# Attention, then two MLPs: the hi and lo rows of q and k written by ScalarE and VectorE instead of by transfers

## The chip, the cores and the metric

One core of one Trainium2 chip runs the whole program. The metric is device time in microseconds (us); the kernel before takes 1175.57 us, the median of 3 runs (1174.51 to 1176.18).

## What is computed

```python
def _attn_ref(q, k, v):                       # 4 batches, 8 heads, 576 rows, 64 columns
    q_rot, k_rot = rotate(q), rotate(k)       # x1*cos - x2*sin, x1*sin + x2*cos
    scores = 1/sqrt(64) * q_rot @ k_rot.T
    attn = exp(scores - max)
    attn = attn / (sum(attn) + 1e-09)
    return attn @ v
def _moe_ref(x, w_gate, w_val, w_out):        # 2304 rows, 512 -> 1536 -> 512
    return (sigmoid(x @ w_gate) * (x @ w_val)) @ w_out
def _moe2_ref(x, w_in, w_out):                # 512 -> 2048 -> 512
    h = x @ w_in
    return (h * sigmoid(1.702 * h)) @ w_out
```

Attention is computed for 32 heads, its output is the input of the first MLP, and that one's output is the input of the second. Everything is float32.

## The kernel before, in words

The program has an attention stage and, behind it, the two MLPs. The change is in the attention stage alone. It works through 16 pairs of heads (pair 0 to 15). For a pair the tile `x` holds q and k of both heads, transposed: partitions 0 to 63 are the 64 columns of head 0, partitions 64 to 127 those of head 1; of its 1152 columns the first 576 are k for head 0 and q for head 1, the last 576 the other way round (`HALVES` names the two). A second tile `xs` holds the same with the two halves of the head's columns exchanged, as the rotation needs them. The rotation is two products and one sum for each half: `rope_mul` on GpSimd, `rope_add` on GpSimd (on VectorE for pair 1).

TensorE multiplies here in a rounded format (fp32r), so each number is split in a rounded part "hi" and the rest "lo", and the product is hi hi + lo lo + lo hi + hi lo. For this a head has a *stack* of 128 partitions, 64 rows of hi and 64 rows of lo (`X` for head 0, `Z` for head 1). One matmul of the stack with itself gives hi hi + lo lo; a second one takes as its weights q's rows exchanged, lo over hi (`Y` for head 0, `Zs` for head 1), and gives the other two products.

`split_qk(i, n)` makes them for pair i: for each half ScalarE writes the rounded part of all 128 partitions to `X` (line 208), and GpSimd the rest to `Y` (line 209; VectorE for pair 1). Both heads' parts then lie on the partitions that the heads have in `x`, and `stack` (lines 258 to 269) moves them to where the matmuls want them by six transfers from SBUF to SBUF, all issued by SyncE. The last two overwrite parts of `Y` and `X` that earlier ones still read, so they wait for these. For pair 0 the function `first_pair` does the same without transfers.

The work of a pair is cut in 9 units (`scores`, lines 271 to 294): 8 units of 128 queries of one head each, and a ninth with the last 64 queries of both heads. A unit's scores fill one of two PSUM buffers `pss`; VectorE takes the maximum (`nm`, line 293), ScalarE the exponentials (line 308), which frees the buffer. Then TensorE transposes them (lines 367 to 379), VectorE or ScalarE copies the result out of PSUM (lines 352 and 354; `PT_DVE` lists the copies that VectorE makes), and TensorE multiplies with v (line 397).

A slot is the work that is recorded around one unit's scores; slot 9 i + u holds unit u of pair i. What else stands in a slot is set by tables of lags: a step of pair i with lag n stands in slot 9 i + n, or 9 i - n for the steps that prepare a pair (`LOAD`, `LOAD_S`, `ROPE_MUL`, `ROPE_ADD`, `SPLIT`). Each engine takes its instructions in the order in which the slots record them; the list `steps` (line 581) says in which order a slot does its steps. During pairs 3 to 8 one piece of the first weights of the MLP is also decoded in each pair (`Weights.decode`, lines 132 to 138: one instruction on ScalarE, five on VectorE, one on GpSimd).

Of the kernel before, what the change touches and what calls it, by code (L numbers as in the profile page):

```python
# [16 lines left out]
P = 128  # L17
# [9 lines left out]
def f(ap):  # L27
    return ap.bitcast(F32)
# [3 lines left out]
def attention_then_mlps(  # L32
# [130 lines left out]
    def load(i, c=slice(0, 2 * S)):  # L163

        if i not in st:
            st[i] = dict(P={}, x=rp.tile([P, 2 * S], F32, tag="x", name="x", bufs=2))
        nc.sync.dma_start(out=st[i]["x"][:, c], in_=qk[i, 0, :, c])

    def load_swapped(i, n, c=slice(0, S)):
# [29 lines left out]
    def rope_add(i, n):  # L199
        add(i, n, nc.gpsimd if i > 1 else nc.vector)  # L200

    def split_qk(i, n):

        if n == 0:
            new_pair(i)
        c = HALVES[n]
        x, hi, lo = (st[i][n_][:, c] for n_ in ("x", "X", "Y"))
        nc.scalar.activation(hi, x, AF.Copy)  # L208
        (nc.gpsimd if i > 1 else nc.vector).tensor_tensor(lo, x, f(hi), ALU.subtract)  # L209
        if n == 1:  # L210
            stack(i)

    def first_pair():


        k, q = HALVES
        q0, q1 = slice(S, S + TAIL + P), slice(S + TAIL + P, 2 * S)
        lo, hi = slice(0, D), slice(D, P)
        first, others = slice(0, TAIL + P), slice(TAIL + P, S)
        for c, n, c_ in ((k, 0, slice(0, S)), (q0, 1, first), (q1, 1, others)):  # L220
            load(0, c)
            nc.scalar.dma_start(out=cos_sin[:, :, c], in_=cos_sin_t[:, :, c])
# [6 lines left out]
        X, Y, Z, Zs = (st[0][n] for n in ("X", "Y", "Z", "Zs"))  # L229
# [17 lines left out]
        hi_of(Zs[hi], x[hi, k])
        hi_of(Y[hi, k], x[hi, q])
        hi_of(Z[lo, k], x[hi, k])
        hi_of(Z[lo, q], x[hi, q])  # L250
        rest(Z[hi, k], x[hi, k], Zs[hi])
        rest(Z[hi, q], x[hi, q], Y[hi, k])
        nc.vector.tensor_copy(Zs[lo], f(Z[hi, k]))
# [247 lines left out]
    LOAD, LOAD_V = 25, -1
    LOAD_S = {ANY: (17, 17), 1: (20, 18), 2: (19, 17)}
# [5 lines left out]
    PT = {ANY: (3, 3, 5, 4, 6, 9, 8, 8, 8, 9, 11, 10, 10, 10), 0: (2, 3, 6, 6, 6, 8, 7, 8, 9, 7, 11, 12, 9, 10), 1: (3, 3, 6, 7, 7, 9, 7, 9, 8, 7, 10, 12, 9, 10), npairs - 1: (3, 3, 6, 6, 5, 8, 7, 9, 8, 7, 12, 12, 9, 11)}  # L508
    PV_STEPS = [(a, [t]) for a in range(2) for t in range(MAINC + 1)]
    PV_EARLY = (0, 7, 8)  # L510
    PV = {ANY: (8, 10, 10, 11, 11, 13, 13, 15, 15, 15), 0: (7, 10, 10, 11, 11, 12, 12, 14, 14, 15), 1: (9, 10, 10, 11, 11, 12, 13, 14, 14, 15), npairs - 1: (8, 9, 10, 11, 11, 15, 16, 17, 17, 18)}

    FACTORS = {ANY: (4, 9), 0: (7, 9)}
    SPREAD = {ANY: (7, 13), 0: (8, 11)}
# [61 lines left out]
    def slot(G):  # L576
# [126 lines left out]
```

## Time and profile before

| | |
|---|---|
| median of 3 runs | 1175.57 us |
| the profiled execution | 1179.7 us |
| its span, from the first to the last instruction | 1177.9 us |
| attention stage, to the first matmul of the MLPs | 337 us |
| MLPs | 841 us |
| busy in the span | TensorE 96%, VectorE 63%, ScalarE 37%, GpSimd 27% |

How to read the rows further down: times are in us unless a row says ns. PE is a matmul on TensorE and PEld its weight load, DVE is VectorE, ACT ScalarE, POOL GpSimd, SPq the queue of SyncE, which issues the transfers. `out<-in` names tiles, without buffer numbers. PEclk is the TensorE clock that the chip granted, 1.00 being 2.4 GHz and 0.50 being 1.2 GHz. A stretch is given as start:end from the start of the span.

### The profile page before, as it was taken

The page shows a single profiled execution, that of the slowest core. Times are in us where ns is not written, and L with a number is a line of the kernel's source. Part 1 is how long each engine was busy: PE and PEld are TensorE (multiplying, and loading weights), DVE is VectorE, ACT ScalarE, POOL GpSimd, SP SyncE. Part 2 cuts the span into 40 slices and gives each one's busy share as a digit, 9 for nine tenths or more (in the row PEclk, how much of TensorE's full clock was granted, in tenths as well). Part 3 has the DMA queues.
Part 4 walks back from the last instruction along what each step waited for, and adds up shares of the span by engine and source line. Part 5 has one row for each costly group of instructions (what it writes and reads, how often), then busy time and mean ns, then how long its engine had stood idle before and what let it go on. Part 6 is the DMA issues. An engine that isn't in the chain of part 4 may idle for free.

```text
span 1177.9 us, 15730 instructions
## 1 busy us (share of the span) xinstructions
PE 1130.3 (96%) x6032; PEld 918.7 (78%) x6032; DVE 742.7 (63%) x1298; ACT 431.5 (37%) x926; POOL 316.4 (27%) x291
## 2 busy tenths in 40 slices
PE   2899898899999999999999999999999999999998
PEld 2576666676778888888888888888888888888887
DVE  6469797665746564655546554567667676676744
ACT  4577677676741121211222112332323222232221
POOL 5577778766211110110100102351001010010100
PEclk9899999999999999999999999999999999999999
DMA  4656565645211111111111111111111111111003
GB/s 173 165 141 180 163 175 149 173 123 141 56 39 52 39 51 36 40 51 36 54 36 38 52 37 36 36 36 52 39 36 55 36 53 38 37 54 36 19 36 125
DMA packets 35275, 86.14 MB, mean 73 GB/s; under 512 B 3952, under 2 KB 4976, under 8 KB 35200
## 3 DMA queue, kind: packets, MB, share of 16 engines
q1 hardware_dynamic: 34352, 83.89, 24.5%
q10 hardware_dynamic: 816, 1.18, 0.3%
q8 instruction: 48, 0.79, 0.3%
q14 instruction: 27, 0.22, 0.1%
q0 software_dynamic: 32, 0.07, 0.0%
HBM read 60.49 MB, written 4.72 MB: 55 GB/s over the span
## 4 chain that ended last, share of the span: by engine, by line
PE 84%; DMA 7%; DVE 2%; ACT 2%; SPq 2%; POOL 2%; issue 1%; ACTq 0%; DVEq 0%; POOLq 0%
PE psh L428 42%; PE pso L428 29%; PE ps_x L397 4%; DMA Zs<-X 4%; PE ps_p L367 3%; PE pss L290 3%; DMA X<-Y 2%; PE pss L291 2%; SPq L269 1%; POOL Y L209 1%; DMA xs<-in_qk_dram 1%; DVE nm L293 1%; PE ps_p L379 1%; ACT P L308 0%; ACT X L208 0%
## 5 line engine op out<-in xcount | busy, mean ns | idle before, releaser
L428 PE MATMUL psh<-xhl,w_in 128*128 128x512 f32 (+1 forms) x2400 | 504.2, 368 | 0.0
L428 PEld LDWEIGHTS psh<-xhl,w_in 128*128 128x128 f32 x2400 | 419.4, 189 | 76.0 <-issue 0.5
L442 ACT ACTIVATE sg<-psh 128x512 f32<-128x512 f32 (+1 forms) x140 | 77.7, 555 | 367.4 <-PE psh L428 366.6
L428 PE MATMUL pso<-w_out,g 128*128 128x512 f32 x864 | 202.4, 389 | 0.0
L444 DVE TENSOR_TENSOR gf<-psh,sg 128x512 f32<-128x512 f32 (+1 forms) x140 | 89.1, 636 | 158.6 <-PE psh L428 112.1
L428 PEld LDWEIGHTS pso<-w_out,g 128*128 128x128 f32 x864 | 161.7, 188 | 33.2
L445 ACT ACTIVATE g<-gf 128x512 fp32r<-128x512 f32 (+1 forms) x140 | 82.5, 589 | 244.0 <-DVE gf L444 244.0
L138 POOL TENSOR_TENSOR w_in<-wt,w_in 128x512 fp32r<-128x512 f32 x40 | 51.8, 1294 | 380.5 <-DVE w_in L137 380.5
L446 DVE TENSOR_TENSOR g<-gf,g 128x512 fp32r<-128x512 f32 (+1 forms) x140 | 95.3, 681 | 91.7 <-ACT g L445 91.7
L428 PE MATMUL pso<-g,w_out 128*128 128x512 f32 (+1 forms) x720 | 152.8, 368 | 0.0
L293 DVE TENSOR_REDUCE nm<-pss 128x1 f32<-128x576 f32 x144 | 107.6, 752 | 58.6 <-PE pss L291 58.1
L428 PEld LDWEIGHTS pso<-g,w_out 128*128 128x128 f32 x720 | 125.8, 189 | 22.6
L138 POOL TENSOR_TENSOR w_out<-wt,w_out 128x512 fp32r<-128x512 f32 x28 | 36.2, 1292 | 263.8 <-DVE w_out L137 263.8
L308 ACT ACTIVATE P<-pss,nm 128x576 f32<-128x576 f32 x128 | 95.1, 743 | 30.0 <-DVE nm L293 29.3
L397 PE MATMUL ps_x<-PT,v 128*64 128x256 f32 (+3 forms) x640 | 102.2, 428 | 0.0
L488 DVE TENSOR_TENSOR acc<-pso,acc 128x512 f32<-128x512 f32 x126 | 83.2, 686 | 20.3 <-PE pso L428 18.0
L367 PE MATMUL ps_p<-ident,P 128*128 128x128 f32 x576 | 86.9, 279 | 0.7 <-ACT P L308 0.7
L290 PE MATMUL pss<-X 128*128 128x288 f32 (+3 forms) x176 | 53.5, 330 | 30.6 <-DMA X<-Y 15.5
L473 DVE TENSOR_TENSOR acc<-pso,acc 128x512 f32<-128x512 f32 (+1 forms) x100 | 61.6, 635 | 28.7 <-PE pso L428 28.7
L354 ACT ACTIVATE PT<-ps_p 128x384 f32<-128x384 f32 (+1 forms) x133 | 62.3, 483 | 44.8 <-PE ps_p L367 39.3
L367 PEld LDWEIGHTS ps_p<-ident,P 128*128 128x128 f32 x576 | 71.3, 144 | 2.7 <-ACT P L308 1.0
L290 PEld LDWEIGHTS pss<-X 128*128 128x128 f32 (+1 forms) x176 | 31.9, 181 | 45.5 <-issue 15.0
(63 smaller groups left out, 1057.2 us busy)
## 6 DMA issues: line engine op xcount, KB each, us to landing
raw<-in_moe_w_out_dram SPq DMA_DIRECT2D x28, 512.0 KB, 3.6
xs<-in_qk_dram SPq DMA_DIRECT2D x31, 288.0 KB, 4.2
x<-in_qk_dram SPq DMA_DIRECT2D x15, 576.0 KB, 4.9
raw<-in_moe_w_in_dram SPq DMA_DIRECT2D x16, 512.0 KB, 3.7
raw<-in_moe_w_gate_dram SPq DMA_DIRECT2D x12, 512.0 KB, 3.8
raw<-in_moe_w_val_dram SPq DMA_DIRECT2D x12, 512.0 KB, 3.8
v<-in_v_dram SPq DMA_DIRECT2D x16, 288.0 KB, 3.8
out_dram<-acc SPq DMA_DIRECT2D x18, 256.0 KB, 2.0
```

Source lines behind the costliest of these rows:

```text
L138: lambda: nc.gpsimd.tensor_tensor(w[:, 1, :], f(t), f(w[:, 0, :]), ALU.subtract),
L290: nc.tensor.matmul(ps[:m, n, o : o + w], T[:, q0 : q0 + m], rhs, start=True, stop=False)
L293: nc.vector.tensor_reduce(nm, ps[:, :, :HALF], axis=AX.XY, op=ALU.max, negate=True)
L308: nc.scalar.activation(st[i]["P"][j][:, c : c + S].rearrange("p (n c) -> p n c", n=2), ps[:, :, :HALF], AF.Exp, bias=nm, accum_out=st[i][" ...
L367: nc.tensor.transpose(ps[:, t * P : (t + 1) * P], pt[:, (3 * g + t) * P : (3 * g + t + 1) * P], ident)
L397: nc.tensor.matmul(ps[h * D : (h + 1) * D, :n], vt[r, vc, :], PT[r, pc, :], start=(t == 0), stop=(t == MAINC))
L428: nc.tensor.matmul(ps, l(sl, a), r(sr, a), start=(sl == 1 and a == 0), stop=(sl + sr == 0 and a == n - 1))
L442: nc.scalar.activation(sg, pss[0][:, :wd], AF.Sigmoid, scale=1.0 if kind == 1 else 1.702)
L444: nc.vector.tensor_tensor(gf, pss[-1][:, :wd], sg, ALU.mult)
L445: nc.scalar.activation(g[:, 0, m, :], gf, AF.Copy)
L446: nc.vector.tensor_tensor(g[:, 1, m, :], gf, f(g[:, 0, m, :]), ALU.subtract)
L488: nc.vector.tensor_tensor(a, ps[:, :DM], a, ALU.add)
```

## The change

`split_qk` works head by head and writes each stack in place. For each head and each half ScalarE writes the rounded part of 64 partitions into the stack's hi rows, and VectorE subtracts and writes the rest into the stack's lo rows, which lie on the other 64 partitions. So a pair has four ScalarE instructions of 64x576 instead of two of 128x576, and four subtractions of 64x576 on VectorE instead of two of 128x576 on GpSimd. `stack` and the tile `Y` are gone. What is left for SyncE are q's exchanged copies, `Xs` and `Zs`: two transfers of 64x576 for each head. `first_pair` is written for the new places of the rows. `x` has three buffers instead of two, and is loaded two slots earlier; the four parts of a split stand in four lags (9, 8, 8 and 5 slots ahead of the pair's first). VectorE makes 4 instead of 6 of the 14 groups of copies out of PSUM, and other lags and the order of the steps in a slot are changed.

```diff
     def load(i, c=slice(0, 2 * S)):
-            st[i] = dict(P={}, x=rp.tile([P, 2 * S], F32, tag="x", name="x", bufs=2))
+            st[i] = dict(P={}, x=rp.tile([P, 2 * S], F32, tag="x", name="x", bufs=3))
...
     def new_pair(i):
-        for n in ("X", "Y", "Z"):
+        for n in ("X", "Z"):
             st[i][n] = rp.tile([P, 2 * S], F32R, tag=n, name=n, bufs=2)
-        st[i]["Zs"] = rp.tile([P, S], F32R, tag="Zs", name="Zs", bufs=2)
+            st[i][n + "s"] = rp.tile([P, S], F32R, tag=n + "s", name=n + "s", bufs=2)
...
+    HEADS = (("X", slice(0, D), slice(D, P), HALVES[1]), ("Z", slice(D, P), slice(0, D), HALVES[0]))
+
     def split_qk(i, n):
         if n == 0:
             new_pair(i)
-        c = HALVES[n]
-        x, hi, lo = (st[i][n_][:, c] for n_ in ("x", "X", "Y"))
-        nc.scalar.activation(hi, x, AF.Copy)
-        (nc.gpsimd if i > 1 else nc.vector).tensor_tensor(lo, x, f(hi), ALU.subtract)
-        if n == 1:
-            stack(i)
+        name, hi, lo, q = HEADS[n // 2]
+        T, Ts, x = st[i][name], st[i][name + "s"], st[i]["x"]
+        c = HALVES[n % 2]
+        nc.scalar.activation(T[hi, c], x[hi, c], AF.Copy)
+        nc.vector.tensor_tensor(T[lo, c], x[hi, c], f(T[hi, c]), ALU.subtract)
+        if HALVES[n % 2] == q:
+            nc.sync.dma_start(out=f(Ts[hi]), in_=f(T[lo, q]))
+            nc.sync.dma_start(out=f(Ts[lo]), in_=f(T[hi, q]))
...
-    def stack(i):
-        X, Y, Z, Zs = (f(st[i][n]) for n in ("X", "Y", "Z", "Zs"))
-        for dst, src in (
-            (Z[0:D], X[D:P]),
-            (Z[D:P], Y[D:P]),
-            (Zs[0:D], Y[D:P, 0:S]),
-            (Zs[D:P], X[D:P, 0:S]),
-            (Y[D:P, S : 2 * S], X[0:D, S : 2 * S]),
-            (X[D:P], Y[0:D]),
-        ):
-            nc.sync.dma_start(out=dst, in_=src)
...
-    PT_DVE = ((0, 1), (2, 0), (2, 2), (3, 1), (4, 0), (4, 1))
+    PT_DVE = ((1, 1), (2, 1), (2, 2), (4, 1))
...
-    LOAD, LOAD_V = 25, -1
+    LOAD, LOAD_V = 27, -1
...
-    ROPE_ADD = {ANY: (13, 10), 1: (8, 7), 2: (12, 9)}
-    SPLIT = {ANY: (8, 7), 1: (6, 5), 2: (8, 8)}
+    ROPE_ADD = {ANY: (12, 10), 1: (9, 8), 2: (12, 9)}
+    SPLIT = {ANY: (9, 8, 8, 5), 1: (6, 5, 5, 4), 2: (8, 8, 7, 7)}
...
-            steps = (step_scores, step_pt, step_decode, step_load, step_pv_early, step_pv, step_rope, step_exps, run_later, step_factors)
+            steps = (step_scores, step_decode, step_load, step_rope, step_pt, step_pv_early, step_exps, step_pv, run_later, step_factors)
```

SyncE, the transfers of one pair in the middle of the stage, of the kernel before. `L269` is `stack`; `x` and `xs` are loads of q and k for later pairs, `v` the load of v, `raw` a piece of the MLP's weights:

```order
L167 DMA x<-in_qk_dram 128x1152
L269 DMA Z<-X 64x1152
L269 DMA Z<-Y 64x1152
L269 DMA Zs<-Y 64x576
L269 DMA Zs<-X 64x576
L269 DMA Y<-X 64x576
L269 DMA X<-Y 64x1152
L111 DMA raw<-in_moe_w_gate_dram 128x2x512
```

The same of the changed kernel, where `L216` and `L217` are the copies of q:

```order
L167 DMA x<-in_qk_dram 128x1152
L111 DMA raw<-in_moe_w_gate_dram 128x2x512
L173 DMA xs<-in_qk_dram 128x576 x2
L184 DMA v<-in_v_dram 128x576
L216 DMA Xs<-X 64x576
L217 DMA Xs<-X 64x576
L216 DMA Zs<-Z 64x576
L217 DMA Zs<-Z 64x576
```

Six transfers became four of the smaller size, and the loads of later pairs now stand ahead of them in the queue.

VectorE in the first three slots of pair 10, of the kernel before. `nm` are the maxima that open the slots, `PT` the copies out of PSUM, `sum` the reciprocal of pair 9's sums, `t` the scaling of an output:

```order
L293 TENSOR_REDUCE nm<-pss 128x1
L321 RECIPROCAL sum<-sum 128x5
L293 TENSOR_REDUCE nm<-pss 128x1
L352 COPY PT_2424<-ps_p 64x64 x2
L352 COPY PT_2424<-ps_p 128x4x64 x2
L293 TENSOR_REDUCE nm<-pss 128x1
L352 COPY PT_2424<-ps_p 128x3x128
```

The same slots of the changed kernel, where `L214` are the subtractions for pair 11:

```order
L286 TENSOR_REDUCE nm<-pss 128x1
L214 TENSOR_TENSOR X<-x,X 64x576
L314 RECIPROCAL sum<-sum 128x5
L286 TENSOR_REDUCE nm<-pss 128x1
L214 TENSOR_TENSOR X<-x,X 64x576
L214 TENSOR_TENSOR Z<-x,Z 64x576
L345 COPY PT_2430<-ps_p 128x4x64 x2
L286 TENSOR_REDUCE nm<-pss 128x1
```

Three subtractions now stand between the maxima of units 0, 1 and 2; the fourth stands in slot 4. Two small copies and one larger one went to ScalarE.

## Rows read from the trace of the kernel before

**Rows 1.** TensorE in order of time: the first and last of 16 matmuls marking unit 8.

```profile
34.93 0.19 PE L290 MATMUL pss<-X 128*64 128x64 f32 x1
...
327.30 0.19 PE L290 MATMUL pss<-X 128*64 128x64 f32 x1
```

**Rows 2.** Busy time by engine of some pairs: us, PE, PEld, DVE, ACT, POOL, PEclk, DMA share, GB/s.

```profile
34.93:60.67 25.74, 20.98 (x129) 14.84 (x127) 11.36 (x23) 14.41 (x40) 14.35 (x15) 0.87 0.64 175
60.67:78.18 17.51, 17.30 (x124) 12.05 (x123) 11.15 (x24) 12.99 (x33) 11.86 (x12) 1.00 0.42 97
78.18:96.29 18.11, 17.52 (x131) 12.75 (x129) 15.43 (x30) 13.91 (x35) 13.31 (x14) 1.00 0.61 178
...
115.19:134.12 18.93, 17.72 (x131) 12.73 (x130) 16.23 (x31) 14.04 (x36) 15.07 (x15) 1.00 0.64 177
...
174.46:193.58 19.12, 17.53 (x130) 12.73 (x129) 15.87 (x31) 13.99 (x36) 14.99 (x15) 1.00 0.61 175
...
212.41:231.11 18.70, 17.25 (x130) 12.71 (x129) 11.95 (x26) 13.41 (x34) 13.32 (x14) 1.00 0.59 151
...
270.48:292.20 21.72, 18.90 (x131) 14.31 (x129) 12.04 (x26) 13.58 (x34) 13.35 (x15) 0.92 0.51 125
292.20:309.41 17.21, 17.21 (x130) 12.72 (x129) 11.94 (x26) 13.39 (x34) 6.40 (x9) 1.00 0.38 90
```

**Rows 3.** Chain of work that ended last, around pair 10's start: start, us, what.

```profile
201.07 0.58 ACT X L208
...
201.72 2.80 POOL Y L209 x2
...
207.04 5.75 DMA Zs<-X
212.84 3.19 DMA X<-Y
...
216.17 0.37 PE pss L290
```

**Rows 4.** Waits, stretch 56:300: who waited for whom, us in total, times, longest.

```profile
PE pss L290 <- DMA X<-Y: 12.1, 7, 2.8
POOL Y L209 <- ACT X L208: 19.4, 17, 3.6
```

**Rows 5.** Short stretches around two waits for the stack, columns as in rows 2.

```profile
235.60:239.20 3.60, 3.53 (x17) 3.55 (x18) 0.93 (x3) 1.41 (x3) 1.41 (x1) 0.56 0.36 132
41.50:47.40 5.90, 5.87 (x25) 4.33 (x25) 2.08 (x4) 3.60 (x11) 1.93 (x2) 0.50 0.34 130
```

**Rows 6.** Durations of the operations that move, ns min/median/max or mean.

```profile
L231 DVE TENSOR_TENSOR Z<-x,Zs x1: 755/755/755, 17.8 to 17.8; 64x576 fp32r<-64x576 f32 x1
L230 ACT ACTIVATE Z<-x x2: 664/672/681, 18.4 to 19.0; 64x576 fp32r<-64x576 f32 x2
L208 ACT ACTIVATE X<-x 128x576 fp32r<-128x576 f32 x2 | 1.4, 704 | 0.0
L209 POOL TENSOR_TENSOR Y<-x,X 128x576 fp32r<-128x576 f32 x2 | 2.8, 1415 | 1.9 <-ACT X L208 1.9
L352 DVE COPY PT<-ps_p 128x384 f32<-128x384 f32 x4 | 2.1, 550 | 0.0
L352 DVE COPY PT<-ps_p 64x64 f32<-64x64 f32 x2 | 0.4, 212 | 0.0
```

**Rows 7.** VectorE with both inputs in SBUF: beside GpSimd's work, and (x62) without it.

```profile
L209 DVE TENSOR_TENSOR Y<-x,X x2: 879/1086/1293, 27.0 to 28.5; 128x576 fp32r<-128x576 f32 x2
L135 DVE SCALAR_TENSOR_TENSOR wt<-raw,wt x6: 681/1823/1830, 92.2 to 189.5; 128x512 uint32<-128x512 uint32 x6
L135 DVE SCALAR_TENSOR_TENSOR wt<-raw,wt x62: 691/693/694, 351.1 to 1115.5; 128x512 uint32<-128x512 uint32 x62
```

**Rows 8.** Transfers of 64x576 by SyncE: count, KB each, us to landing.

```profile
Zs<-X SPq DMA_DIRECT2D x15, 144.0 KB, 5.6
Y<-X SPq DMA_DIRECT2D x15, 144.0 KB, 2.3
```

More of the change, by code (lines that the diff above doesn't have):

```diff
@@ L228, in first_pair @@
         x = st[0]["x"]
-        X, Y, Z, Zs = (st[0][n] for n in ("X", "Y", "Z", "Zs"))
+        X, Xs, Z, Zs = (st[0][n] for n in ("X", "Xs", "Z", "Zs"))
         hi_of = lambda dst, src: nc.scalar.activation(dst, src, AF.Copy)
@@ L241, in first_pair @@
         rest(X[hi, k], x[lo, k], X[lo, k])
-        hi_of(Y[hi, q0], x[lo, q0])
+        hi_of(Xs[hi, first], x[lo, q0])
         rest(X[hi, q0], x[lo, q0], X[lo, q0])
-        nc.vector.tensor_copy(Y[lo, q0], f(X[hi, q0]))
+        nc.vector.tensor_copy(Xs[lo, first], f(X[hi, q0]))
         rope(q1, 1, others, nc.gpsimd)
[L247 to L253, printed above, removed]
-        rest(X[hi, q1], x[lo, q1], X[lo, q1])
-        nc.vector.tensor_copy(Y[lo, q1], f(X[hi, q1]))
-        hi_of(Y[hi, q1], x[lo, q1])
-    def stack(i):
-        X, Y, Z, Zs = (f(st[i][n]) for n in ("X", "Y", "Z", "Zs"))
-        for dst, src in (
-            (Z[0:D], X[D:P]),
-            (Z[D:P], Y[D:P]),
-            (Zs[0:D], Y[D:P, 0:S]),
-            (Zs[D:P], X[D:P, 0:S]),
-            (Y[D:P, S : 2 * S], X[0:D, S : 2 * S]),
-            (X[D:P], Y[0:D]),
-        ):
-            nc.sync.dma_start(out=dst, in_=src)
+        hi_of(Z[hi, k], x[hi, k])
+        hi_of(Zs[lo], x[hi, k])
+        hi_of(Z[hi, q], x[hi, q])
+        rest(Z[lo, k], x[hi, k], Z[hi, k])
+        rest(Z[lo, q], x[hi, q], Z[hi, q])
+        nc.vector.tensor_copy(Zs[hi], f(Z[lo, k]))
+        rest(X[hi, q1], x[lo, q1], X[lo, q1])
+        nc.vector.tensor_copy(Xs[lo, others], f(X[hi, q1]))
+        hi_of(Xs[hi, others], x[lo, q1])
     def scores(i, u):
@@ L276, in scores @@
         for h_ in (h,) if j < MAINC else (1, 0):
-            T, Qs = (st[i][n] for n in (("X", "Y"), ("Z", "Zs"))[h_])
+            T, Qs = (st[i][n] for n in (("X", "Xs"), ("Z", "Zs"))[h_])
             m, cols = P, [(0, 0, 0, HALF), (1, 0, HALF, HALF)]
@@ L282, in scores @@
                 q0, k0 = j * P, S
+            qs = HEADS[h_][3].start
             if j == MAINC:
@@ L290, in scores @@
                 nc.tensor.matmul(ps[:m, n, o : o + w], T[:, q0 : q0 + m], rhs, start=True, stop=False)
-                nc.tensor.matmul(ps[:m, n, o : o + w], Qs[:, q0 : q0 + m], rhs, start=False, stop=True)
+                nc.tensor.matmul(ps[:m, n, o : o + w], Qs[:, q0 - qs : q0 - qs + m], rhs, start=False, stop=True)
         nm = st[i]["nm"][:, h, j : j + 1]
@@ L500, in attention_then_mlps @@
     ANY = None
[L501 to L502 removed]
+    LOAD, LOAD_V = 27, -1
+    LOAD_S = {ANY: (17, 17), 1: (20, 17), 2: (20, 18)}
     ROPE_MUL = {ANY: (17, 20, 13, 14), 1: (17, 20, 13, 13), 2: (17, 20, 13, 12)}
[L504 to L505 removed]
+    ROPE_ADD = {ANY: (12, 10), 1: (9, 8), 2: (12, 9)}
+    SPLIT = {ANY: (9, 8, 8, 5), 1: (6, 5, 5, 4), 2: (8, 8, 7, 7)}
     PT_STEPS = [(j, g) for j in range(MAINC) for g in range(3)] + [(MAINC, 0), (MAINC, 1)]
[L508 removed]
+    PT = {ANY: (3, 3, 5, 6, 6, 7, 7, 8, 7, 9, 10, 11, 11, 10), 0: (2, 5, 6, 5, 7, 9, 7, 8, 9, 7, 11, 12, 9, 10), 1: (3, 3, 6, 7, 6, 9, 7, 11, 8, 7, 10, 12, 9, 10), npairs - 1: (3, 3, 6, 6, 5, 8, 7, 9, 7, 7, 12, 13, 10, 10)}
     PV_STEPS = [(a, [t]) for a in range(2) for t in range(MAINC + 1)]
[L510 to L511 removed]
+    PV_EARLY = (0, 1, 7)
+    PV = {ANY: (9, 9, 9, 11, 11, 13, 13, 15, 15, 15), 0: (7, 10, 10, 11, 11, 12, 12, 14, 14, 15), 1: (9, 10, 10, 11, 11, 13, 13, 14, 14, 14), npairs - 1: (8, 9, 11, 11, 11, 14, 15, 16, 16, 16)}
     FACTORS = {ANY: (4, 9), 0: (7, 9)}
[L514 removed]
+    SPREAD = {ANY: (8, 13), 0: (8, 10)}
     DEC_PAIR, DEC_UNIT = (3, 1)
```

## The prediction

> **What bounds the kernel now.** I looked first at where the change can act. The MLPs take 841 of the 1177.9 us and hold none of the changed lines, so everything is decided in the first 337 us. I then cut this stage into pairs. Unit 8 of each pair has one matmul of 64 columns on 64 partitions that no other unit has, so its 16 starts mark the pairs [rows 1]: from 34.93 us (pair 0) to 327.30 us (pair 15), 292.4 us for 15 pairs, 19.5 us each. Below, "the stretch of pair i" runs from the mark of pair i-1 to that of pair i.
>
> The stretches tell what is slow [rows 2]. Pair 14 takes 17.21 us and TensorE is busy in all of it: this is the pace at which nothing but TensorE limits. Pair 2 takes 17.51 us. The others are longer: 18.7 to 19.1 us where nothing else happens, over 21 us in three stretches of which pair 13's is shown (pairs 6 and 11 are the others), 25.74 us in pair 1. No other engine fills those stretches: in pair 10 VectorE is busy 11.95 of 18.70 us, ScalarE 13.41, GpSimd 13.32.
>
> The chain of waits names the cause [rows 3]. Around the start of pair 10 it runs ScalarE's rounding, 2.80 us of GpSimd's subtractions, the transfers up to `Zs<-X` (5.75 us), `X<-Y` (3.19 us), and then the first matmul of the next pair. The rounding stands two slots into a pair and its result is wanted at the next pair's first slot, so this is a ring with a fixed length of about 18.7 us. The engines catch up in each pair and wait at its end. TensorE's direct waits for `X<-Y` look small, 12.1 us in 7 times [rows 4], but the time in which it ran short of work ahead of them comes on top: it was busy 17.25 of pair 10's 18.70 us.
>
> A wait can cost a second time [rows 5]. Behind two of them, at 41.5 us and 235.6 us, the granted clock was 0.50 and 0.56 (the 1.2 GHz level, wholly or nearly) for 5.9 and 3.6 us. What such a stretch loses is its length times the missing share of the clock, 5.9 x 0.50 = 3.0 and 3.6 x 0.44 = 1.6 us. The long stretches of pairs 6 and 13 have the same sign, a mean clock of 0.92 where pair 10 has 1.00.
>
> **The change part by part, in one pair.** *Taken away:* six transfers, 3 x 288 and 3 x 144 KB, and the two dependent steps among them; two GpSimd subtractions, 2 x 1.415 = 2.83 us [rows 6]. *Added:* four transfers of 144 KB. Such a transfer lands 2.3 us after its issue where little is queued and 5.6 us where much is [rows 8]. In the changed order those for `Xs` and `Zs` stand behind slot 1's subtractions, some 3 to 5 us into a pair; with four issues and the larger landing time they end 11 to 12 us into it, and the next pair begins after 17. I cost them at nothing, with 5 us of cover. The loads now ahead of them in SyncE's queue wait for buffers that are free pairs earlier (the third `x`), so they don't hold them.
>
> *VectorE:* four subtractions of 64x576 that change partitions, 0.755 us each [rows 6], +3.0; less one copy of 0.55 and two of 0.21, -1.0. So 11.95 becomes 14.0 us in pair 10 and 16.23 becomes 18.3 us in pair 4, where a piece of weights is decoded [rows 2]. *ScalarE:* four of 0.672 for two of 0.704 is +1.3; the copies it takes over cost 0.5 and 2 x 0.2 at VectorE's durations: 13.41 becomes 15.6 us. *GpSimd:* 13.32 becomes 10.5 us.
>
> What does a subtraction wait for on VectorE that it did not on GpSimd? The trace has few of these, so I bound it. Pair 1's two (there VectorE does it) took 0.88 and 1.29 us, beside a GpSimd at work without a break [rows 7]: 0.13 and 0.54 us over the undisturbed 0.755. A decode instruction with two SBUF inputs took 0.69 us in the MLPs and mostly 1.82 us here [rows 7]; its excess of 1.13 us is nearly a whole GpSimd instruction (1.41). So the wait lies between 0 and 1.4 us. I take 0.2, nearest to pair 1's two (0.33 in the mean), scaled down because GpSimd will be busy some 0.65 of the time: 0.8 us a pair.
>
> The Trainium skill bears on this (SBUF — State Buffer, section "Who interferes with whom"): it says that a VectorE instruction with two SBUF inputs and a GpSimd instruction that reads SBUF exclude each other, and that whichever comes second waits for the whole of the first. The 1.82 us agree with that, the 0.88 us do not show a full wait. By the rule, met by every subtraction in full, the sum comes to the first rival's 1206 us instead of 1157.
>
> *The start:* pair 0's slots get pair 1's four roundings and four subtractions in place of two and two, while TensorE waits there anyway; half of 2 x 0.67 + 2 x 0.755 us is +0.7, taken as +0.8 (between 0 and 1.5). Pair 1 then starts without the wait that ended at 41.5 us, and without the slow clock behind it. I give it 18.3 us: pair 2's 17.51 plus one subtraction, as pair 2's split (two subtractions in each of two slots) falls into it; bounds 17.2 and 25.7.
>
> **The sum, by stretches.** Pair 0 +0.8. Pair 1 from 25.74 to 18.3: -7.4. Pair 2 from 17.51 to 17.7: +0.2. Pairs 3 to 8, the six with decoding, take 115.4 us now (78.18 to 193.58). VectorE's 18.3 us are above TensorE's 17.2, so it limits. Its decode instructions should wait less for a GpSimd that has 12.2 instead of 15.1 us to do, its subtractions wait 0.8: I take 18.7 us each, 112.2, -3.2 (bounds 17.3 and 21.0, which is 18.3 plus the 2.7 us that VectorE idles in pair 4 now). Pairs 9 to 13 take 98.6 us now (193.58 to 292.20). All other engines end well below TensorE (ScalarE 15.6, VectorE 14.8), so TensorE's 17.2 plus 0.4 for short waits in crowded slots, 17.6 each, 88.0, -10.6 (bounds 17.2 and 18.7). Pairs 14 and 15 +0.2; the rest as it is. Together **-20.0 us**.
>
> The profiled execution took 1179.7 us, 4.1 above the median of the runs. Taken from it the sum gives 1159.7, from the median 1155.6. The 4.1 us may be a price of profiling, which stays, or slow-clock stretches that unprofiled runs have fewer of, which would shrink the gain; I put the forecast between, at **1157 us**.
>
> **Rivals.** *Slower: VectorE and GpSimd block each other.* With b us of waiting in each subtraction, VectorE needs 18.3 + 4b in pairs 3 to 8 and 14.0 + 4b in the others. The loss 6 x (18.3 + 4b - 18.7) eats the gain of 20 at b = 0.9; beyond that the kernel is slower. At 1.4, a whole GpSimd instruction each time, pairs 3 to 8 need 23.9 and the rest 19.6: +31 and 9 x 2 = +18 on the forecast, 1206 us. For it: the 1.82 us [rows 7]. Against: GpSimd's load falls, and in slot 0 it mostly waits for the sums itself.
>
> *VectorE stands behind ScalarE.* A subtraction needs the rounding just ahead of it. On GpSimd that wait was 19.4 us in all, some 0.7 us for each of its 26 subtractions there (pairs 3 to 15, two each) [rows 4], and cost nothing; VectorE has the next unit's maximum queued behind it, for which ScalarE and then TensorE wait. 4 x 0.7 on 18.3 is 21.1 us: pairs 3 to 8 lose 2.4 each against the forecast, 14 us, giving 1171. In the others 14.0 + 2.8 = 16.8 stays under TensorE's pace. For it: slot 1 would hold some 3 us of VectorE work for 1.9 us of slot. Against: the wait is shorter when VectorE comes late.
>
> *TensorE's pace everywhere.* If VectorE's work in pairs 3 to 8 packs without gaps, or its decode instructions lose their waits, all 15 pairs take 17.3 us: 259.5 for 292.4, 1143 us.
>
> *The transfers stay on the path.* If SyncE reaches the copies late because a load ahead of them waits, the period stays near 18.7 us and only pair 1 and one or two slow-clock stretches are won: -9, 1167 us. The 5 us of cover speak against it.
>
> **How the numbers follow.** The forecast's case 0.62 (1150 to 1165); VectorE behind ScalarE 0.13; blocking to the point of a loss 0.12; TensorE's pace everywhere 0.08; transfers still late 0.05. About 0.2% (2.4 us) is what a measurement of this kernel can tell from no change. Faster is the first case and the fourth, 0.09 of the second and 0.03 of the fifth: 0.82. The upper ends of the second and fifth give 0.05 for no change and 0.01 for slower, the blocking 0.12 more: 0.13. The range runs from 1146, most of the way to TensorE's pace, to 1176, where the blocking begins to cost more than the change saves.
>
> **What the profile after would show.** Right: no wait of TensorE for a transfer of `Xs` or `Zs`; clock 1.00 from pair 1 on; pairs 9 to 13 near 17.6 us with TensorE above 97% busy; pairs 3 to 8 near 18.7 with VectorE the busiest share of its stretch; pair 1's mark near 54 us. Wrong: subtractions over 1.7 us in the mean (blocking), VectorE idle ahead of them for ScalarE by 0.5 us and more each, or slow clock in new places, which would mean that TensorE's waits were moved and not removed.

## The result, and the profile after

The changed kernel takes **1185.11 us**, the median of 4 runs (1183.66 to 1186.0), beside 1175.88 us for the kernel before (4 runs, 1174.51 to 1176.91). The ratio is 1.0078 (95% interval 1.0061 to 1.0096): it is slower by 0.8%, where 1157 us were forecast. Its profiled execution took 1185.72 us with a span of 1183.5; that of before took 1179.7 and 1177.9. The two spans differ by 5.6 us and the medians by 9.2, since the profiled execution of before was about 4 us longer than that kernel's median.

The marks of the pairs, of the changed kernel (TensorE in order of time, as in [rows 1]; unit 8's first matmul is now on line 283):

```profile
38.08 0.19 PE L283 MATMUL pss<-X 128*64 128x64 f32 x1
...
333.14 0.19 PE L283 MATMUL pss<-X 128*64 128x64 f32 x1
```

All 15 stretches between them take 295.1 us (292.4 before). By the steps of the forecast, in us:

| stage | before | forecast | measured | measured - before |
|---|---|---|---|---|
| pair 0, to its mark | 34.9 | 35.7 | 38.1 | +3.2 |
| pair 1 | 25.7 | 18.3 | 18.8 | -7.0 |
| pair 2 | 17.5 | 17.7 | 19.2 | +1.7 |
| pairs 3 to 8, with decoding | 115.4 | 112.2 | 128.2 | +12.8 |
| pair 9 | 18.8 | 17.6 | 22.3 | +3.5 |
| pairs 10 to 13 | 79.8 | 70.4 | 71.8 | -8.0 |
| pairs 14, 15 | 35.1 | 35.3 | 34.8 | -0.3 |
| to the MLPs, and the MLPs | 850.6 | 850.6 | 850.4 | -0.2 |

Pairs 1 and 10 to 13 won 15.0 us; pair 0, pair 2, the pairs with decoding and the one behind them lost 21.2. The busy times by engine, of the changed kernel (columns as in [rows 2]; the stretches are pairs 1, 2, 4, 6, 9 and 11, and two short ones in pair 4):

```profile
38.08:56.84 18.76, 17.73 (x127) 12.65 (x125) 13.03 (x24) 15.41 (x42) 7.78 (x10) 1.00 0.48 148
56.84:76.08 19.24, 18.36 (x134) 13.31 (x132) 15.28 (x27) 15.48 (x41) 10.47 (x11) 1.00 0.34 104
95.24:120.72 25.48, 20.70 (x131) 14.19 (x129) 20.15 (x34) 17.06 (x44) 13.60 (x14) 0.87 0.43 136
140.75:161.80 21.05, 18.27 (x130) 12.85 (x129) 17.90 (x32) 15.92 (x42) 12.96 (x13) 1.00 0.41 127
204.28:226.56 22.28, 19.10 (x131) 13.83 (x129) 15.87 (x29) 16.47 (x43) 13.96 (x15) 0.92 0.32 95
244.51:262.47 17.96, 17.36 (x131) 12.83 (x130) 13.98 (x27) 15.36 (x40) 11.71 (x12) 1.00 0.40 117
112.00:115.00 3.00, 0.75 (x6) 0.55 (x5) 2.92 (x6) 0.79 (x2) 1.04 (x1) 0.93 0.15 17
115.00:118.00 3.00, 3.00 (x13) 1.11 (x13) 2.65 (x5) 2.04 (x5) 0.00 (x0) 0.50 0.74 225
```

Pair 11 shows what was meant: TensorE is busy 17.36 of 17.96 us, and VectorE's 13.98 is the forecast's 14.0. In pair 6 VectorE's 17.90 is also near the forecast's 18.3; yet the stretch is 21.05 us long, and VectorE idles in 3.15 of them. No engine fills it, which points to a ring again. In pair 4 TensorE stands for most of 3 us and then runs at a granted clock of 0.50 (the 1.2 GHz level) for the next 3, as before behind other waits [rows 5].

The waits of the changed kernel in the stretch 56:300 (as [rows 4]):

```profile
DVE sum L314 <- POOL sum L312: 8.2, 5, 1.6
...
DVE X L214 <- ACT X L213: 6.1, 12, 0.8
...
DVE Z L214 <- ACT Z L213: 5.5, 6, 1.4
PE ps_p L360 <- DVE rb L334: 3.0, 2, 2.2
```

TensorE's wait for a transfer of a stack is gone; no matmul waits for any transfer any more. VectorE waits for GpSimd: line 312 adds 1e-9 to the sums on GpSimd, line 314 takes their reciprocal on VectorE. That wait is not new: the kernel before had as much of it (`DVE sum L321 <- POOL sum L319: 7.9, 9, 1.6`). New is the ring that it now closes; the chain of waits through pair 6 shows it (columns as in [rows 3]):

```profile
139.77 0.41 DVE t L405
...
140.20 0.37 ACT xhl L409
...
140.64 1.19 POOL xhl L411 x2
141.84 1.38 POOL x L190
143.21 1.23 POOL w_in L138
144.45 1.90 POOL x L194
...
146.43 0.25 POOL sum L312
...
146.70 0.20 DVE sum L314
...
148.20 0.76 DVE X L214
...
148.99 0.75 DVE Z L214
...
154.01 1.12 DVE wt L134
...
155.15 0.75 DVE Z L214
...
157.58 1.52 DVE wt L135
...
160.37 0.47 DVE PT L345
160.83 0.41 DVE t L405
```

It starts at VectorE's `t` (an output of an earlier pair, scaled) and ends 21.06 us later at the next `t`: the period of pairs 6 and 7. GpSimd must wait for `t` and its rounding, then has the output's rest, a product, a decode subtraction and a rotation sum in its queue ahead of the tiny addition. VectorE waits there for 1.6 us, has its subtractions and decode instructions behind it, and so comes late to `t`. Two kinds of pieces are longer than they need be. The sum on line 194 took 1.90 us, 1.41 undisturbed. And VectorE's decode instructions, of the changed kernel (durations as in [rows 7], in ns, with the subtractions):

```profile
L134 DVE TENSOR_SCALAR wt<-wc x6: 416/1205/1467, 87.4 to 197.2; 128x512 uint32<-128x512 uint32 x6
L135 DVE SCALAR_TENSOR_TENSOR wt<-raw,wt x6: 680/1606/1609, 90.9 to 200.0; 128x512 uint32<-128x512 uint32 x6
...
L214 DVE TENSOR_TENSOR X<-x,X x26: 751/753/1739, 59.9 to 303.7; 64x576 fp32r<-64x576 f32 x26
L214 DVE TENSOR_TENSOR Z<-x,Z x26: 753/754/1975, 63.3 to 310.0; 64x576 fp32r<-64x576 f32 x26
```

Half the subtractions or more take the undisturbed 0.75 us, and their mean excess is 0.10 us (means 0.821 and 0.879). Lines 134 and 135 together lose (1.205 - 0.416) + (1.606 - 0.680) = 1.7 us a pair to GpSimd (run e5 below shows that it is GpSimd).

At the start, in pair 0, GpSimd went on from 16.69 us without a break for the pairs to come (the third buffer of `x` lets it begin on pair 2), and VectorE worked beside it (timelines of VectorE and of GpSimd, changed kernel: start, us, what, and in brackets the idle time before):

```profile
16.75 3.82 DVE L237 TENSOR_TENSOR Z<-x,Z 64x576 fp32r<-64x576 f32 x2 [1.28 <-ACT Z L236]
...
16.69 3.27 POOL L190 TENSOR_TENSOR x<-x,cos_sin 128x576 f32<-128x576 f32 x2
```

The two subtractions took 3.82 us; [rows 6] has 0.755 for one.

### The profile page after: what moved, and what is told of

Same layout as the page of the kernel before. It is cut to its first block, busy times and chain, and to the rows that moved or that the text cites. A ratio compares the mean times of both kernels' runs of the same rounds, so it can differ in the third digit from the quotient of the medians.

```text
span 1183.5 us, 15769 instructions
## 1 busy us (share of the span) xinstructions
PE 1132.1 (96%) x6032; PEld 918.9 (78%) x6032; DVE 776.8 (66%) x1311; ACT 460.5 (39%) x1000; POOL 288.3 (24%) x263
## 4 chain that ended last, share of the span: by engine, by line
PE 82%; DVE 8%; ACT 5%; POOL 3%; issue 1%; DMA 1%; SPq 0%; ACTq 0%; DVEq 0%
PE psh L421 42%; PE pso L421 29%; PE ps_x L390 4%; PE ps_p L360 2%; PE pss L283 2%; DVE nm L286 2%; PE pss L284 2%; DVE Z L214 1%; ACT P L301 1%; ACT X L213 1%; POOL x L194 1%; ACT PT L347 1%; POOL x L190 1%; ACT Z L213 1%; DVE wt L135 1%
## 5 line engine op out<-in xcount | busy, mean ns | idle before, releaser
L437 DVE TENSOR_TENSOR gf<-psh,sg 128x512 f32<-128x512 f32 (+1 forms) x140 | 89.0, 635 | 158.9 <-PE psh L421 112.2
L481 DVE TENSOR_TENSOR acc<-pso,acc 128x512 f32<-128x512 f32 x126 | 83.1, 686 | 20.2 <-PE pso L421 18.0
L347 ACT ACTIVATE PT<-ps_p 128x384 f32<-128x384 f32 (+1 forms) x178 | 71.6, 432 | 4.4 <-PE ps_p L360 3.6
L390 PEld LDWEIGHTS ps_x<-PT,v 128*64 128x64 f32 (+1 forms) x640 | 38.4, 137 | 39.6 <-issue 23.4
```

The costliest lines, as they stand in the source:

```text
L390: nc.tensor.matmul(ps[h * D : (h + 1) * D, :n], vt[r, vc, :], PT[r, pc, :], start=(t == 0), stop=(t == MAINC))
L437: nc.vector.tensor_tensor(gf, pss[-1][:, :wd], sg, ALU.mult)
L481: nc.vector.tensor_tensor(a, ps[:, :DM], a, ALU.add)
```

## The experiments

The theory after the result: VectorE and GpSimd exclude each other for whole instructions (**the lock**), and GpSimd's queue ties VectorE's end of a pair to its beginning (**the ring**). The rival theories: VectorE is simply full in pairs 3 to 8; the new order of slots costs it; the early loads at the start cost it. The kernel of each run is the changed one unless "before" is said. The columns by pair are of each run's profiled execution; the last is the median, and for e3, e5 and e8 a single execution. Ratios are to executions of the kernel before on the same chip.

| run | pair 0's mark | pairs 3 to 8, each | pair 9 | pairs 10 to 13, each | first MLP matmul | us |
|---|---|---|---|---|---|---|
| before | 34.9 | 19.2 | 18.8 | 20.0 | 336.9 | 1175.88 |
| changed | 38.1 | 21.4 | 22.3 | 18.0 | 342.7 | 1185.11 |
| e1, no addition | 38.7 | 20.2 | 20.1 | 19.9 | 342.3 | 1185.06 |
| e2, GpSimd's decoding later | 40.0 | 20.2 | 19.8 | 18.0 | 336.5 | 1178.1 |
| e3, decoding behind | 39.3 | 18.0 | 18.0 | 18.0 | 325.5 | 1187.04 |
| e8, the same of before | 36.8 | 18.7 | 18.9 | 18.8 | 335.7 | 1196.71 |
| e4, GpSimd held at the start | 40.3 | 21.2 | 19.6 | 18.0 | 341.3 | 1184.94 |
| e5, no rotation | 40.4 | 18.3 | 17.9 | 18.0 | 322.9 | 1165.53 |
| e6, subtractions on GpSimd | 40.2 | 22.8 | 22.3 | 19.8 | 362.7 | 1204.48 |
| e7, decoding spread | 39.9 | 19.4 | 19.7 | 19.6 | 336.3 | 1181.3 |
| e9, two pieces in the MLP | 40.1 | 20.5 | 18.0 | 18.0 | 335.7 | 1178.56 |
| e10, the same of before | 37.6 | 18.8 | 18.9 | 18.9 | 330.0 | 1173.94 |
| e11, e9 and e2 | 39.4 | 19.7 | 18.0 | 18.0 | 330.0 | 1172.8 |
| e12, and ScalarE rounds | 39.5 | 19.7 | 18.0 | 18.0 | 331.1 | 1172.34 |

### The ring's link: the addition left out

```diff
     def factors(i, a):
-        nc.gpsimd.tensor_scalar_add(s, s, 1e-9)
```

> The changed kernel without GpSimd's addition of 1e-9 to the sums (a sum holds exp(0) = 1, and 1 + 1e-9 is 1 in float32, so the values are the same). Theory 'ring through GpSimd': in pairs 3 to 8 VectorE waits 1.6 us per pair for this small instruction, which stands at the end of GpSimd's queue behind 1.2 us of output splits, 1.4 us of a product, 1.2 us of decoding and 1.9 us of a sum of the rotation, and the whole closes to a ring of 21.1 us. Without it these pairs fall to 18.5 to 19.5 us, and the kernel gains 10 to 15 us on the changed one. Rival 'VectorE is full': it is busy 17.9 of 21.1 us and the rest are gaps of many small waits; the pairs stay within 0.4 us of 21.1 and the kernel gains under 3 us. Pairs 10 to 14 stay at 17.95 us by both.

1185.06 us, ratio 1.0098 (1.0077 to 1.0120). The decoding pairs fell by 0.8 us to 20.3 in the middle, less than expected, the pairs without decoding *rose* from 17.96 to 19.9, and the kernel won nothing. The busy times of pair 6 and pair 11 of this run:

```profile
137.36:157.67 20.31, 17.80 (x130) 12.85 (x129) 18.62 (x32) 16.07 (x41) 12.72 (x11) 1.00 0.42 133
238.25:258.17 19.92, 17.50 (x131) 12.83 (x130) 15.92 (x27) 15.37 (x40) 10.52 (x10) 1.00 0.36 107
```

In pair 11 VectorE is busy 15.92 us with 27 instructions; the changed kernel's pair 11 has 27 too, in 13.98. The first subtraction of the pair in the timelines of this run, with GpSimd's product, and behind it the same two of the changed kernel:

```profile
241.29 1.61 DVE L214 TENSOR_TENSOR X<-x,X 64x576 fp32r<-64x576 f32 x1
...
240.87 1.42 POOL L190 TENSOR_TENSOR xs<-xs,cos_sin 128x576 f32<-128x576 f32 x1
```

```profile
247.55 0.75 DVE L214 TENSOR_TENSOR X<-x,X 64x576 fp32r<-64x576 f32 x1
...
247.57 2.01 POOL L190 TENSOR_TENSOR xs<-xs,cos_sin 128x576 f32<-128x576 f32 x1
```

Here GpSimd's product began 0.42 us ahead of the subtraction, and that was over at 242.90, 0.61 us behind the product's end. In the changed kernel the subtraction came 0.02 us ahead, and the product took 0.6 us longer. Who comes second waits. Without the addition GpSimd no longer stood still in front of it, arrived first and blocked VectorE, on which TensorE's next unit depends: the small addition, a link of the ring in pairs 3 to 8, had kept GpSimd out of the way in the others.

Nor did the decoding pairs lose their ring. The longest pieces of the chain of waits through pair 6 of this run:

```profile
137.89 1.39 POOL x L190
139.28 1.23 POOL w_in L138
140.51 1.93 POOL x L194
143.18 1.25 DVE X L214
150.26 1.86 DVE Z L214
```

The chain starts at a `t` at 135.82 us and comes to the next one 20.31 us later. On GpSimd it runs over the same product, decode subtraction and rotation sum (line 194) as in the changed kernel; from there it now goes over ScalarE's rounding of the rotated rows to VectorE's subtraction. One link of the ring was taken out, and another one, almost as late, closes it.

### GpSimd's piece of the decoding three slots later

```diff
         if dec:
             dec.pop(0)()
+        for op in late.pop(G, ()):
+            op()
...
-                    dec += wts[1, 0].decode(i - DEC_PAIR)
+                    ops = wts[1, 0].decode(i - DEC_PAIR)
+                    dec += ops[:-1]
+                    late[G + len(ops) + 3] = [ops[-1]]
```

> The changed kernel with GpSimd's decode instruction (1.27 us) recorded three slots later, behind the addition to the sums. Ring theory: the chain from the output split to the reciprocal is 1.2 us shorter, so pairs 3 to 8 fall by 1.2 us or more, to 19 to 20 us, and the kernel gains 6 to 12 us. 'VectorE is full': GpSimd's order does not matter, the pairs stay near 21.1 us.

1178.1 us, ratio 1.0033 (1.0022 to 1.0044), where the changed kernel had 1.0078; one instruction's place was worth some 5 us, less than the 6 to 12 expected. Decoding pairs took 20.4 us, the others kept 17.96. The clock is 1.00 from pair 2 on, so the slow stretches that the changed kernel has in pairs 4, 8 and 9 are gone too.

### No decoding in the pairs, changed and before

```diff
-            if DEC_PAIR <= i < DEC_PAIR + wts[1, 0].n:
...
+        for i in range(wts[1, 0].n):
+            wts[1, 0].load(i)
+            for op in wts[1, 0].decode(i):
+                op()
         rot.close()
```

> The changed kernel with the six pieces decoded behind the attention stage instead of in pairs 3 to 8. Both theories: all pairs from 2 on near 17.95 us, the attention's last matmul some 20 us earlier; the decoding, now with nothing beside it, costs 15 to 30 us behind. If pairs 3 to 8 stay above 19 us, the decoding is not what makes them long, and the subtractions themselves are.

> The kernel before with the decoding behind the attention stage, as in experiment 3. If its period is the ring of transfers, as the prediction read it, pairs 3 to 8 keep 18.5 to 19 us without the decoding, and the changed kernel without decoding (17.96 us a pair) is 0.7 us and more faster in each. If VectorE's load sets it, the pairs fall to 17.5 us.

With the decoding behind the attention loop, the changed kernel's pairs 3 to 13 take 18.0 us each, pairs 4 and 9 too (pair 2 stays at 19.3). The kernel before keeps 18.5 to 19.4 us in eight of its pairs 4 to 13 without the decoding (17.2 in pair 3, 18.0 in pair 4, 20.8 in pair 7), with VectorE busy 12 us or less in each. So it was not the decoding or VectorE's load that bounded before, as the reading of a ring of transfers has it; the change removes that bound, and with the decoding gone the changed pairs are no longer long. Without decoding in the loop the changed kernel reaches the MLPs 10.2 us earlier (325.5 to 335.7) and is 9.7 us faster (one execution of each). Both totals rise, as the six pieces then stand bare ahead of the MLPs (15.6 us from the last mark instead of 9.5) and the MLP stage takes 859 instead of 841 us.

### No early start for GpSimd

```diff
+            if G == -3:
+                g = sp.tile([P, 1], F32, name="gate")
+                nc.gpsimd.tensor_scalar_add(g[0:D], f(st[0]["Xs"][0:D, S - 1 : S]), 1.0)
             slot(G)
```

> The changed kernel with one tiny GpSimd instruction that reads the last rows VectorE writes for pair 0, recorded ahead of GpSimd's products for pair 2, so that these start at about 23 us, as they did before the change, and not at 18. Theory 'early load': the third buffer let GpSimd start pair 2 while VectorE made pair 0's subtractions, and these lost 3 us to it (two took 3.82 instead of 1.43 us). Then unit 8 of pair 0 comes 2 to 3 us earlier than 38.1, and the kernel gains 2 to 3 us. Rival 'more work in pair 0': the two more roundings and subtractions in slots 3 to 5 cost the 3 us; the mark stays within 1 us of 38.1, or pair 1 and 2 get later by what pair 0 gains.

1184.94 us: nothing won. Pair 0's two subtractions ran undisturbed (0.75 us each), but GpSimd's products then met a sum of pair 1's rotation on VectorE (line 194: 2.97 us, 0.76 in the changed kernel), and the mark came at 40.3 us instead of 38.1. Runs e1, e2, e3, e6, e7 and e9 have pair 0's lines unchanged, and there the two happened not to collide (0.75 us each); their marks, at 38.7 to 40.2 us, are no earlier. That the collision at 16.75 us makes pair 0 late is refuted.

### No rotation on GpSimd

The products and sums of the rotation are left out from pair 4 on, so q and k stay unrotated there:

```diff
     def rope_mul(i, n):
-        mul(i, 1 - n % 2, n // 2, nc.gpsimd)
+        if i < 4:
+            mul(i, 1 - n % 2, n // 2, nc.gpsimd)
```

(and the same for `rope_add`)

> The changed kernel without GpSimd's products and sums of the rotation from pair 4 on (q and k of these pairs stay unrotated): GpSimd keeps only the output splits, the sums' additions and the decode instruction, some 4 of a pair's 21 us, and VectorE's own instructions are the same. Theory 'lock' (a VectorE instruction with both inputs in SBUF and a GpSimd instruction wait for each other): VectorE's decode instructions and subtractions lose their waits of 2 to 3 us a pair, and pairs 5 to 8 fall from 21.1 to 18 to 18.7 us. Theory 'VectorE is full' (its own work and the maxima's deadlines): the same instructions in the same order, so the pairs stay above 19.8 us. The ring through the sums' addition is opened here too; experiment 1, where it alone was opened, gave 20.3 us, so what falls below that is not the ring.

Decoding pairs take 18.3 us (one execution of the kernel: 1165.53 us). The busy times of pair 6 and the decode instructions of that run:

```profile
133.79:152.11 18.32, 17.59 (x130) 12.86 (x129) 16.25 (x32) 15.93 (x41) 3.61 (x7) 1.00 0.47 149
```

```profile
L134 DVE TENSOR_SCALAR wt<-wc x6: 416/417/417, 89.8 to 181.5; 128x512 uint32<-128x512 uint32 x6
L135 DVE SCALAR_TENSOR_TENSOR wt<-raw,wt x6: 681/681/681, 93.2 to 184.8; 128x512 uint32<-128x512 uint32 x6
```

VectorE executes 32 instructions in 16.25 us, 2.4 less than the 32 of run e1's pair 6 took. So it is not full, and the pairs are not long because of the new order: the 2 us between 20.3 and 18.3 go with GpSimd's rotation, and both decode instructions named above are back at their undisturbed time.

The expectation says that what falls below e1's 20.3 us is not the ring. That does not follow: e1's ring ran over the rotation's sum, so this run took the lock and that link away together. How the 2 us divide between them, no run shows.

### Subtractions back on GpSimd

```diff
-        nc.vector.tensor_tensor(T[lo, c], x[hi, c], f(T[hi, c]), ALU.subtract)
+        (nc.gpsimd if i > 1 else nc.vector).tensor_tensor(T[lo, c], x[hi, c], f(T[hi, c]), ALU.subtract)
```

> The changed kernel with the subtractions back on GpSimd from pair 2 on (four of 64x576), the direct writes and the four transfers kept. If it is the move to VectorE that costs, VectorE loses 3.0 us and its waits, pairs 3 to 8 fall below 20 us; GpSimd gets 4 x 1.41 = 5.6 us, 17.3 us in the other pairs and 18.7 in pairs 3 to 8, which it then limits: 18.0 to 18.5 and 19 to 20 us, the kernel 1165 to 1178 us. If GpSimd's order (its head waits for the output splits, 6 to 11 us a pair) is the limit, the pairs get longer than now, 20 us and more everywhere, and the kernel 1195 us or more.

1204.48 us, ratio 1.0248 (1.0228 to 1.0269), the slowest. GpSimd's subtraction in this run:

```profile
L214 POOL TENSOR_TENSOR X<-x,X x9: 1394/1402/1408, 104.5 to 197.0; 64x576 fp32r<-64x576 f32 x9
```

On 64 partitions it takes 1.40 us, as on 128 [rows 6]: the new layout doubles GpSimd's work for the split. Pairs 4 to 8 take 23 us with GpSimd busy 17.6 to 17.8 of them; the chain of waits there goes through GpSimd's queue, and through loads as well. With this layout the move to VectorE is right.

### Decoding spread over two pairs

```diff
-                    dec += wts[1, 0].decode(i - DEC_PAIR)
+                    for op in wts[1, 0].decode(p):
+                        dec.extend([op] + [lambda: None] * 1)
```

(pieces in pairs 2, 4, ... 12, one decode step in every second slot)

> The changed kernel with each piece's decoding spread over two pairs (one instruction in every second slot, pieces in pairs 2, 4, ... 12). VectorE then needs some 16 to 17 us a pair. If pairs 3 to 8 are long because the subtractions and the decoding don't fit into one pair of VectorE beside GpSimd, by lock or by load, all pairs from 3 on come to 18.0 to 18.6 us, without slow clock, and the kernel to 1158 to 1166 us, faster than before the change. If any decode instruction in a pair closes a ring, pairs 3 to 13 all stay above 19.5 us and the kernel is slower than the changed one.

1181.3 us, ratio 1.0062 (1.0039 to 1.0086). Twelve pairs take 18.6 and 19.7 us in turn, 38.3 for two; that is what a pair of 20.4 and one of 17.96 take. Two pairs had slow clock (21.4 and 21.7 us). Spreading moved the loss and did not shrink it; neither of the two expected cases came.

### The last two pieces decoded in the MLP

`w_out`'s two pieces are first needed behind the first block's hidden layer, so their decoding can go beside it.

```diff
-            if DEC_PAIR <= i < DEC_PAIR + wts[1, 0].n:
+            if DEC_PAIR <= i < DEC_PAIR + wts[1, 0].n_in:
...
+                if at == n == 0:
+                    for i in range(W.n_in, W.n):
+                        W.load(i)
                 g = hidden(kind, W, n)
+                if at == n == 0:
+                    for i in range(W.n_in, W.n):
+                        for op in W.decode(i):
+                            op()
```

> The changed kernel with the last two of the six decoded pieces (w_out's) loaded and decoded in the MLP's first block instead of in pairs 7 and 8. Lock theory (VectorE's decode instructions and GpSimd's sums exclude each other only where a piece is decoded): pairs 7 and 8 fall from 21.2 us to 17.96 and the tail that pair 9 has (22.3) moves to pair 7, so about 6.5 us less in the attention stage, and 0 to 3 us more in the MLP's first block: 1179 to 1182 us. Rival, that the pairs 3 to 8 are long for another reason that stands in those slots (the loads, the order of the slots): pairs 7 and 8 stay near 21, 1185 us.

> The kernel before with the same move of w_out's two pieces. Its pairs are held by the ring of transfers with or without decoding (18.7 to 19.1 us both), so the move is worth nothing there: pairs 7 and 8 stay at 18.5 to 19.0, and the time stays within 0.3% of before or rises by up to 3 us for the decoding in the MLP's first block. If decoding cost the kernel before as much as it costs the changed one, it would win 5 us or more.

The changed kernel falls to 1178.56 us (1.0031; 1.0021 to 1.0041), some 5 us less than without the move by the ratios. Pairs 3 to 6 keep theirs (21.1 in the middle), pair 7 takes the tail (22.3) and pair 8 is at 17.95. The kernel before takes 1173.94 us (0.9989; 0.9978 to 0.9999), some 1 us less (2.6 at most). Decoding cost the changed kernel what it did not cost the kernel before.

### Both moves, and one instruction less on VectorE

```diff
-                lambda: V.tensor_copy(w[:, 0, :], f(t)),
+                lambda: nc.scalar.activation(w[:, 0, :], f(t), AF.Copy),
```

(in the attention stage, in e12 alone; e11 has e2's and e9's edits, e12 all three)

> The changed kernel with w_out's two pieces in the MLP and, for the four pieces left, GpSimd's instruction of the decoding three slots later. From the run with that delay alone (20.4 us in a decoding pair, 19.8 in the one behind the last): 4 x 20.4 + 19.8 + 17.96 in place of 6 x 20.4, so some 4 us under that run's 1178.1, 1173 to 1176 us, level with the kernel before. If the move only shifts the loss into the MLP, 1178.

> The same, and the decoding's rounding of the piece (SBUF to SBUF, 0.42 us on VectorE undisturbed, 0.77 where GpSimd blocks it) is made by ScalarE in the attention stage. Lock theory: one instruction fewer in each decoding pair that can be locked out, 0.4 to 0.8 us less in each of four pairs, 1170 to 1174 us, under the kernel before. Rival, that ScalarE (15.9 us of a decoding pair) takes over the limit: decoding pairs no shorter than 20.4 us, 1174 to 1177.

e11 takes 1172.8 us (0.9980; 0.9969 to 0.9991), e12 1172.34 (0.9983; 0.9973 to 0.9993): both under the kernel before by 0.2%, and level with e10, the kernel before with one of the moves. e12's decoding pairs stay at 20.4 us: VectorE is busy 18.3 instead of 19.2 us in them, and idles that much more for TensorE. The rounding took 0.77 us in the changed kernel and no less in e5, so GpSimd's rotation was not what held it up (0.43 us in the MLPs), and what VectorE gained it waited away. The 0.4 to 0.8 us a pair that the lock theory expected did not come.

## Why the prediction was wrong

- **The step "I take 18.7 us each, 112.2, -3.2" for pairs 3 to 8 failed**, and with it pair 9: +12.8 and +3.5 us. Their mean of 21.4 us lies outside the step's own bounds too (17.3 to 21.0). The load was right (18.3 forecast, 17.9 measured in pair 6), and VectorE was taken as the limit because its load was above TensorE's. But an engine that both waits and is waited for is not done when its load is done: it idled 3.15 of 21.05 us. What the runs showed in its place, by taking one thing away after the other: 21.1 us; 20.3 without the link over the small addition (e1); 18.3 without GpSimd's rotation (e5); 17.96 without decoding (e3). So of the 3.1 us that a decoding pair is too long, about 0.8 goes with that link, 2.0 with GpSimd's rotation (VectorE's instructions took 2.4 us less without it) and 0.4 with the decoding's load. The 2.0 are lock and ring together; an estimate of the lock's part comes from the pieces of pair 6's chain, which are longer than undisturbed by 0.5 us (line 194), 0.8 and 0.9 us (lines 134 and 135), 2.2 us of 21.06. The slow clock in pairs 4, 8 and 9 comes on top, the "slow clock in new places" that the prediction named as a sign of being wrong: mean clocks of 0.87, 0.92 and 0.92, by its own reckoning 3.3, 1.7 and 1.8 us. In pair 4 one such stretch, 3 us at half clock, stands behind a wait of 2.2 us for a copy that VectorE made late, behind decode instructions of 1.42 and 1.47 us and a subtraction of 1.84.
- **The clue was in the rows.** [Rows 7] had a decode instruction at 1.82 us instead of 0.69. I read it only as a bound for the *subtractions* and assumed that the decode instructions would wait less. They waited as before: lines 134 and 135 lost 1.7 us a pair in both kernels (0.97 and 1.82 us before, 1.21 and 1.61 after). In the kernel before VectorE had time for it; 16.23 busy us stood in 18.93 (the row 115.19:134.12, which the prediction calls pair 4 and which is pair 5). After the change it has not.
- **The rival "VectorE and GpSimd block each other"** named the right mechanism and the right sign at the wrong place: it asked for 0.9 us of waiting in each subtraction, and they wait 0.10. Nor did it see that GpSimd waits too (1.90 and 2.01 for 1.41 us): its load was 11.71 us in pair 11 for the 10.5 forecast. The Trainium skill (SBUF — State Buffer, section "Who interferes with whom") has both: that the second to come is locked out for the whole of the other's instruction, and that the order of issue decides which side waits. Run e1 agrees, with 1.61 against 0.75 us for the same subtraction.
- **"VectorE stands behind ScalarE"**: its waits ahead of the subtractions are 6.1 us over 12 times for `X` and 5.5 over 6 for `Z`, 0.6 us each where they occur, but only at 18 of 48 subtractions. In e5 they remain (13.3 us over 26 times), and the pairs take 17.9 to 18.3 us all the same.
- **Pair 1, -7.4**: right (-7.0); clock 1.00, no wait for a stack.
- **Pairs 9 to 13 at 17.6**: pairs 10 to 13 took 17.95, -8.0 for the forecast's -9.4 there. The missing 0.35 us is not the lock: e5 has 18.0 as well.
- **Pair 0 and pair 2, +0.8 and +0.2**: they took +3.2 and +1.7. The collision at 16.75 us is shown, that it is the cause is not (e4). In the other runs of the changed kernel pair 0's mark came at 38.7 to 40.4 us; before, and its two variants, had it at 34.9 to 37.6. So the price, some 3 us, is real. The timelines of VectorE show where the larger part arises (changed kernel):

```profile
29.13 0.76 DVE L286 TENSOR_REDUCE nm<-pss 128x1 f32<-128x576 f32 x1
29.92 1.06 DVE L214 TENSOR_TENSOR X<-x,X 64x576 fp32r<-64x576 f32 x1
31.01 1.85 DVE L214 TENSOR_TENSOR Z<-x,Z 64x576 fp32r<-64x576 f32 x1
32.79 0.74 DVE L286 TENSOR_REDUCE nm<-pss 128x1 f32<-128x576 f32 x1
```

  Between the fifth and the sixth maximum VectorE makes two of pair 1's subtractions, longer than 0.75 us beside GpSimd's products. These two maxima stand 3.7 us apart in the changed kernel and all its variants, 1.9 us in the kernel before and its two variants: 1.8 us of the 3.2. The prediction's term took half of what the added instructions need undisturbed, and no wait. No run removed it, and the rest stays open. Of pair 2's +1.7 us, 0.9 went with GpSimd's rotation (18.3 us in e5).
- **The base.** I started between the profiled execution and the median. The profiled execution of before held slow-clock stretches that another execution may not have: e10's profile, of nearly the same kernel, at 1172.81 us, has no pair from 3 to 13 over 19.9 us where that of before had three of 21 to 22. So a part of the gain counted in pairs 9 to 13 was likely there only in the profiled execution.

The forecast's sum closes: -20.0, and +2.4 in pair 0, +0.5 in pair 1, +1.5 in pair 2, +16.0 in pairs 3 to 8, +4.7 in pair 9, +1.4 in pairs 10 to 13 and -0.8 in the rest give +5.7 for the 5.6 us by which the spans differ.

## What to carry to other kernels

When work moves to an engine, don't compare loads alone. Follow the engine's queue once around the period: what it waits for, and what comes late behind it, on the other engine too. On a pair of engines that lock each other out, look for every instruction of both sides that is already longer than it is elsewhere in the trace, and price it again with the slack gone. And where one stage carries extra work (here the decoding), ask first whether that work must stand there: moving a third of it brought some 5 us, and so did another place for one instruction.

## What was not expected of the hardware

The lock's price depends on tiny shifts: removing an instruction of 0.25 us (e1) turned the same subtraction from 0.75 to 1.61 us and made four undisturbed pairs 1.95 us longer each. A decode instruction with a *single* SBUF input (line 134, `tensor_scalar` on 128x512 uint32) was blocked nearly as much as one with two: 1.205 us in the median for 0.416, where line 135 took 1.606 for 0.680. And GpSimd's elementwise subtraction takes 1.40 us on 64 partitions, as long as on 128.
